# First key loads and packs split over two DMA queues, and two changes to a planner's clock, in an attention and mixture-of-experts kernel

## The chip, the cores and the metric

One Trainium2 chip, one of its cores. The metric is device time in microseconds (us) of one execution, as the median of several runs. Before the change it is 415.95 us, the median of 3 runs from 412.87 to 416.46.

## What is computed

There are 8 batches of 8 heads, 576 tokens and a head size of 64, all in float32. Per batch, 32 pack vectors `p` attend over keys `k` and values `v`, and then the queries `q` attend over the 32 packed results. The output of that, 576 x 512, goes through a mixture of 8 experts: one expert per token, two layers (512 to 1024 with a ReLU, 1024 to 512), scaled by the gate's probability.

```python
p_packed = softmax(scale * p @ k.T) @ v            # per batch and head, 32 x 64
x = softmax(scale * q @ p_packed.T) @ p_packed      # 576 x 64 per head, 576 x 512 per batch
logits = x @ w_gate; local = sigmoid(x @ w_local)
for s in range(576):                                # per batch
    fresh = argmax(logits[s])
    e = fresh if s == 0 or local[s] < 0.5 else e    # expert of this token
    out[s] = softmax(logits[s])[e] * (relu(x[s] @ w1[e]) @ w2[e])
```

The inputs are random, with `q`, `k` and `p` of spread 0.8 and small gate weights.

## The kernel before

**Work.** The kernel takes the expert of a batch's first token for the whole batch, counts tokens that would have another one, and has a branch behind the main program for those. Per batch, tokens are turned so that the head dimension lies on partitions; the scores of packs against keys are made (line 504), softened on VectorE and ScalarE (512 to 533), turned (542, 547), multiplied with the values (568) and turned again into `ppT` (589). Then come the scores of queries against `ppT` (619) and their softmax (654 to 686), which leaves the weights of the 32 packs for each token as a rounded part `a2h` and a rest `a2l`. The first layer's weights `w1` of the chosen expert are multiplied with `ppT` (941 for batch 0, in quarters; 970 for the others, in two halves of 512 columns), so that the first layer works on `a2h` and `a2l` directly (1012). Its result goes through ReLU into `h` (1023, 1027) and the second layer (1045, 1050, 1054), in 2 x 8 chunks a batch. Stores are at 1094.

**The order of the work.** It is written out when the program is built. Each piece is a generator that yields `need(...)`: the tiles it waits for, banks of PSUM and conditions. A planner, `weave`, keeps a clock of its own (`Clock`), whose `note` gives every emitted instruction a start and an end on its engine; a piece is taken when the clock says that what it needs is there, and the chunks (`main`) come when nothing of the attention pieces is due. As long as `warm_ps` is held, which is until batch 0's third chunk, a stretch in which the clock finds nothing ready is filled with multiplications of constants, `keep_warm` (line 228, tile `heat`), one for each 230 ns. Every engine runs its instructions in the order in which they were emitted; what they truly wait for are semaphores, which the clock does not decide.

**What the clock believes.** A DMA ends after its bytes over a rate, plus 2000 or 2500 ns (line 165). SP's and ScalarE's transfers are two lines that do not slow each other. A tile has one time of writing, or two where `halves` lists it; an instruction that writes a tile starts after the last write of it, by whatever engine, and after the last use.

**Around the change.** `loads` for batch 0 issues the packs (line 373: the same rows twice, to the left and the right half of `p_in`, one from SP and one from ScalarE), then the small inputs (299, 300, 302: two batches' first queries, `w_local`, `w_gate`, all from ScalarE), and then on SP the keys of Q 0 (347, in two pieces of two heads, and 349, the tail of 64 tokens, tile `qt`), the keys of Q 1, the values (330, 332) and the queries. Q numbers the two groups of four heads. `turn_tokens` turns keys: two groups of four transposes (449), copied to the tile `xT` (named `qn`) by ScalarE and by VectorE (451), one transpose of the tail (457) and its copy by ScalarE (459). The three copies write different columns. `turn_small` (309, 311) turns the small inputs and is taken once Q 0's keys are turned. `weights` loads `w1` (904 for batch 0, 920 for the others, two transfers of 1 MB each) and `w2` (891), once the expert is in a register. `pack_weights` (970) needs both halves of `w1`.

Of the kernel before, what the change touches and what calls it, by code (L numbers as in the profile page):

```python
# [19 lines left out]
B, H, S, D = 8, 8, 576, 64  # L20
# [5 lines left out]
NJ = 4  # L26
# [30 lines left out]
PICK = 2  # L57
# [3 lines left out]
class Clock:  # L61
# [3 lines left out]
    def __init__(self):  # L65
        self.until, self.written, self.used, self.before = {}, {}, {}, {}
        self.slots, self.done, self.group, self.tiled, self.products = {}, set(), (None, set()), False, 0.0

        self.halves = {}

        self.rate = 300.0

        self.port = {"DVE": [], "Pool": []}

# [58 lines left out]
    def note(self, inst):  # L133
        outs = [x.bass_ap for x in inst.outs if hasattr(x, "bass_ap")]
        ins = [x.bass_ap for x in inst.ins if hasattr(x, "bass_ap")]
        if inst.opcode == "TensorLoad":

            if "SP" in str(inst.engine):
                self.until["SP"] = self.ready([x for x in ins]) + 1000.0
        if not outs:  # L140
            return
        dma = inst.opcode == "DMACopy"
        if dma:
            aside = "Activation" in str(inst.engine)
            kind, took = "DMA2" if aside else "DMA", min(x.free_size() * x.partition_size() for x in outs + ins if x.space != DRAM) * 4 / self.rate
        else:
            kind, took = self.price(inst, outs, ins)
        start = max(self.engine(kind), self.engine("Activation" if aside else "SP") if dma else 0.0)
        for x in ins + ([] if dma else outs):
            at, by = self.written.get(self.key(x), (0.0, kind))  # L150
            start = max(start, at + (LAT if by != kind else 0.0 if kind == "PE" else SAME))
        for x in outs:
            t = x.tensor.name
            start = max(start, 0.0 if dma else self.used.get(self.key(x), 0.0))
            if t in self.before:
                start = max(start, self.used.get(self.before.pop(t), 0.0) + LAT)
        if kind == "Pool" or kind == "DVE" and inst.opcode in ("TensorTensor", "TensorScalar", "TensorScalarPtr") and not any(x.space == PSUM for x in ins + outs):
            for a, z in self.port["DVE" if kind == "Pool" else "Pool"][-8:]:
                if a <= start < z:
                    start = z  # L160
            self.port[kind].append((start, start + took))
        end = start + took
        self.until[kind] = end
        if dma:
            end += 2000.0 if start < 25000.0 else 2500.0
        for x in outs:
            self.written[self.key(x)] = (end, kind)
        for x in ins + outs:
            for t in {x.tensor.name, self.key(x)}:
                self.used[t] = max(end, self.used.get(t, 0.0))  # L170
# [3 lines left out]
def packed_attn_moe_kernel(  # L174
# [12 lines left out]
    nc = tc.nc  # L187
# [4 lines left out]
    clock = Clock()  # L192
    at_batch = [-1]

    def tile_(shape, dtype, name, tag=None):
        bufs = BUFS.get(tag or name, 2)
        x = sb.tile(shape, dtype, name=name, tag=tag or name, bufs=bufs)
        clock.follow(x.tensor.name, tag or name, bufs)
        return x
# [42 lines left out]
    small = const.tile([(PICK + 1) * H, D], F32, name="small")  # L242
# [53 lines left out]
    def load_small():  # L296

        clock.rate = 100.0
        nc.scalar.dma_start(out=small[0:PICK * H], in_=q[0:PICK, :, 0, :].rearrange("b h d -> (b h) d"))
        nc.scalar.dma_start(out=small[PICK * H:(PICK + 1) * H], in_=w_local.rearrange("(h d) e -> h (d e)", d=D))  # L300
        sts[0]["rows"] = tile_([128, DM], F32, "gate_rows", "w2raw")
        nc.scalar.dma_start(out=sts[0]["rows"][0:H], in_=w_gate.rearrange("(h d) e -> h (d e)", d=D))

    def turn_small():

# [29 lines left out]
    def load_pairs(st, name, Q):  # L335

        src, b, tag = (k if name == "k" else q), st["b"], "kv" if name == "q" and st["second"] else "w2s"
        x = tile_([128, HQ, NJ * D], F32, "kv" if tag == "kv" else "kw", tag)
        clock.halves[x.tensor.name] = HQ * NJ * D
        if Q == 0:  # L340
            st[name, "rest"] = tile_([128, NQ, 2 * D], F32, "qt", "o")
            clock.halves[st[name, "rest"].tensor.name] = NQ * 2 * D
        rest = st[name, "rest"][:, Q]
        rows = at(src, b).rearrange("(h q) s d -> q h s d", q=NQ)[Q]
        clock.rate = 300.0
        for hs in (slice(0, 2), slice(2, 4)) if st["early"] and (name, Q) == ("k", 0) else (slice(0, 4),):
            nc.sync.dma_start(out=x[:, hs], in_=rows[hs, 0:512].rearrange("h (p c) d -> p h (c d)", c=NJ))
        clock.rate = 200.0
        nc.sync.dma_start(out=rest, in_=rows[:, 512:S].rearrange("h (p r) d -> h p (r d)", r=2))
        return x, rest  # L350
# [17 lines left out]
    def load_packs(b, queues):  # L368

        x = tile_([128, 2, 2 * D], F32, "p_in")  # L370
        clock.rate = 400.0
        for z, queue in enumerate(queues):
            queue.dma_start(out=x[:, :, D * z:D * z + D], in_=at(p, b).rearrange("(g h) n d -> (h n) g d", g=2))
        return x
# [23 lines left out]
    def loads(st):  # L398

        b = st["b"]  # L400
        if st["early"]:
            st["px"] = load_packs(b, (nc.sync, nc.scalar))
            load_small()

            order = (("k", 0), ("k", 1), ("v", 0), ("v", 1), ("q", 0), ("q", 1))
        else:
            if isinstance(b, int):
                yield need(when=lambda: "loaded" in sts[b - 1] and (b < 2 or "ereg" in sts[b - 2]))
            order = (("k", 0), ("k", 1), ("p", 1)) if st["second"] else \
                (("v", 0), ("v", 1), ("p", 1), ("k", 1), ("q", 1))  # L410
        for name, Q in order:
            blocks = name in "kq" and not st["pairs"]
            if isinstance(b, int) and b > 1:
                yield need(when=lambda: all(len(sts[x].get(y, ())) == n for x, y, n in ((b - 2, "w2", NC), (b - 1, "w1", 2)) if "ereg" in sts[x]))
# [21 lines left out]
    def turn_tokens(st, name):  # L436
# [2 lines left out]
        yield need(slot="qn", when=lambda: (name, 0) in st and (early or ("a2t" in st if st["early"] else sts[0]["asked"] >= NQ)))  # L439
        xT = st[name] = tile_([128, NQ, HQ, HALF], F32, "qn")  # L440
        clock.halves[xT.tensor.name] = H * HALF
        for Q in range(NQ):
            yield need(when=lambda: (name, Q) in st and (early and (Q == 0 or st["scored"] > 0) or st["second"] or st["valued"] == NQ and (Q == 0 or st["ppT"][Q] is not None)))
            x, rest = st[name, Q]
# [436 lines left out]
    def weights(st):  # L881
# [34 lines left out]
        for fh in range(2):  # L916
            yield need(slot="w1t")
            clock.rate = 330.0
            w1t = tile_([128, HQ, 512], F32, "w1t")
            nc.sync.dma_start(out=w1t, in_=src[:, :, 512 * fh:512 * fh + 512])  # L920
            st["w1"].append(w1t)
        for c in range(NC):
            yield from second(c)
# [436 lines left out]
```

## Time and profile before

| what | value |
|---|---|
| median of 3 runs | 415.95 us (412.87 to 416.46) |
| time of the profiled execution | 415.69 us |
| its span in the trace | 413.9 us |
| TensorE (PE) busy | 405.7 us, 98% |
| VectorE (DVE) busy | 301.9 us, 73% |
| ScalarE (ACT) busy | 180.1 us, 44% |
| moved by DMA | 73.08 MB, mean 177 GB/s |
| mean granted TensorE clock | 0.998 of full speed |

Times in the trace count from the start of the span. PE are TensorE's multiplications, PEld its weight loads, which lie beside them; SPq and ACTq are the sequencers of SyncE and ScalarE, which issue DMAs. A line such as L970 is one of the kernel before. "Idle before" is the time that an engine stood still before an instruction, with what ended it. The chain of waits is the work that ended last, followed back step by step.

### The profile page before, as it was taken

What the parts mean: (1) busy time and instruction counts of PE and PEld (TensorE: products, weight loads), DVE (VectorE), ACT (ScalarE), POOL (GpSimd) and SP (SyncE); (2) the same over time, 40 slices, a digit from 0 to 9 for tenths busy, and PEclk for the clock granted to TensorE, in tenths of its full rate; (3) what the DMA queues carried; (4) which work ended last, traced back from release to release, by engine and by line L of the source; (5) the groups of instructions that cost most, each with busy time, mean ns of one, the idle gap of its engine ahead of it and who ended that gap; (6) DMA issues with size and microseconds to landing.
All of it is one profiled execution on the core that took longest, in us unless ns stands there. A gap on an engine that the chain in (4) does not pass through costs nothing.

```text
span 413.9 us, 10072 instructions
## 1 busy us (share of the span) xinstructions
PE 405.7 (98%) x3820; PEld 319.8 (77%) x3821; DVE 301.9 (73%) x905; ACT 180.1 (44%) x440; POOL 47.7 (12%) x67
## 2 busy tenths in 40 slices
PE   7999999999999999999999999999999999999995
PEld 4657787678868778788787788877787788878895
DVE  2498779895868949697588968878597976867231
ACT  2556543653436424446245443355244453454221
POOL 2003500641030000300002000300003000110000
PEclk9999999999999999999999999999999999999999
DMA  7869998999994997849994799938998400733021
GB/s 219 254 230 319 121 187 246 210 255 169 137 329 138 229 143 124 306 132 209 127 234 181 236 155 141 319 111 226 126 146 303 153 2 2 272 122 129 0 66 55
DMA packets 169325, 73.08 MB, mean 177 GB/s; under 512 B 135088, under 2 KB 149424, under 8 KB 169272
## 3 DMA queue, kind: packets, MB, share of 16 engines
q1 hardware_dynamic: 168792, 72.17, 79.9%
q8 instruction: 31, 0.51, 0.6%
q10 hardware_dynamic: 480, 0.22, 0.2%
q14 instruction: 22, 0.18, 0.2%
HBM read 62.94 MB, written 9.44 MB: 175 GB/s over the span
## 4 chain that ended last, share of the span: by engine, by line
PE 91%; DMA 5%; ACT 1%; SPq 1%; DVE 0%; issue 0%; DVEq 0%; ACTq 0%
PE bank L1045 41%; PE bank L1012 24%; DMA w1t<-in_moe_w_dram 4%; PE bank L1050 4%; PE bank L1054 4%; PE bank L970 3%; PE bank L568 2%; PE bank L504 2%; PE bank L619 2%; PE bank L542 2%; PE bank L228 2%; DMA qt<-in_k_dram 1%; PE bank L797 1%; PE bank L449 1%; PE bank L941 1%; PE bank L739 1%
## 5 line engine op out<-in xcount | busy, mean ns | idle before, releaser
L1045 PE MATMUL bank<-w2s,h 128*128 128x512 f32 (+1 forms) x792 | 204.6, 392 | 0.0
L1045 PEld LDWEIGHTS bank<-w2s,h 128*128 128x128 f32 x792 | 137.2, 188 | 25.8 <-issue 3.1
L1023 ACT ACTIVATE h<-bank 128x256 fp32r<-128x256 f32 (+1 forms) x128 | 52.7, 412 | 111.5 <-PE bank L1012 110.7
L1027 DVE SCALAR_TENSOR_TENSOR h<-bank,h 128x256 fp32r<-128x256 f32 x192 | 61.7, 349 | 52.7 <-ACT h L1023 51.1
L1012 PEld LDWEIGHTS bank<-a2h,wph 128*128 128x128 f32 x256 | 46.1, 188 | 19.7 <-issue 5.6
L686 POOL TENSOR_TENSOR a2l<-a2t,a2h 128x576 fp32r<-128x576 f32 (+2 forms) x17 | 24.1, 1419 | 300.6 <-ACT a2h L683 300.6
L1012 PE MATMUL bank<-a2h,wph 128*128 128x320 f32 (+1 forms) x256 | 56.5, 302 | 0.1
L1012 PE MATMUL bank<-a2h,wpl 128*128 128x320 f32 (+1 forms) x256 | 54.6, 294 | 0.0
L1012 PE MATMUL bank<-a2l,wph 128*128 128x320 f32 (+1 forms) x256 | 54.3, 293 | 0.0
L1012 PEld LDWEIGHTS bank<-a2h,wpl 128*128 128x128 f32 x256 | 40.8, 188 | 0.3
L1012 PEld LDWEIGHTS bank<-a2l,wph 128*128 128x128 f32 x256 | 40.8, 188 | 0.0
L998 ACT CAST w2s<-w2raw 128x512 fp32r<-128x512 f32 x64 | 38.5, 621 | 3.8 <-DMA w2raw<-in_moe_w_dram 3.8
L1000 DVE TENSOR_TENSOR w2s<-w2raw,w2s 128x512 fp32r<-128x512 f32 x50 | 33.3, 679 | 0.0
L1050 PE MATMUL bank<-w2s,h 128*128 128x512 f32 x64 | 26.9, 420 | 0.0
L1054 PE MATMUL bank<-w2s,h 128*64 128x512 f32 x64 | 25.2, 394 | 0.0
L985 DVE TENSOR_TENSOR wpl<-bank,wph 128x512 fp32r<-128x512 f32 x28 | 18.2, 682 | 7.8 <-ACT wph L982 7.8
L982 ACT CAST wph<-bank 128x512 fp32r<-128x512 f32 x28 | 15.1, 593 | 18.1 <-PE bank L970 18.1
L639 DVE STREAM_TRANSPOSE sT<-bank 128x288 f32<-128x288 f32 (+2 forms) x36 | 13.0, 418 | 9.7 <-ACT gate L637 9.0
L1000 POOL TENSOR_TENSOR w2s<-w2raw,w2s 128x512 fp32r<-128x512 f32 x14 | 18.1, 1309 | 14.1 <-ACT w2s L998 5.8
L603 DVE STREAM_TRANSPOSE qn<-qn 128x1152 f32<-128x1152 f32 x14 | 19.2, 1368 | 0.0
L471 DVE STREAM_TRANSPOSE qn<-qn 128x1152 f32<-128x1152 f32 x12 | 16.3, 1362 | 0.0
L512 DVE TENSOR_SCALAR_CACHE_REDUCE a<-bank 128x288 f32<-128x288 f32 x32 | 13.3, 453 | 3.0 <-PE bank L504 3.0
(158 smaller groups left out, 457.3 us busy)
## 6 DMA issues: line engine op xcount, KB each, us to landing
w2raw<-in_moe_w_dram SPq DMA_DIRECT2D x64, 256.0 KB, 5.7
w1t<-in_moe_w_dram SPq DMA_DIRECT2D x14, 1024.0 KB, 7.2
kv<-in_v_dram SPq DMA_DIRECT2D x16, 512.0 KB, 5.8
qn<-in_q_dram SPq DMA_DIRECT2D x28, 288.0 KB, 6.7
out_dram<-o SPq DMA_DIRECT2D x28, 256.0 KB, 3.5
qn<-in_k_dram SPq DMA_DIRECT2D x24, 288.0 KB, 7.4
w1t<-in_moe_w_dram SPq DMA_DIRECT2D x4, 512.0 KB, 4.7
out_dram<-o SPq DMA_DIRECT2D x14, 128.0 KB, 2.4
```

The lines of the kernel that those rows point to most:

```text
L471: nc.vector.transpose(out=kT, in_=kT)
L603: nc.vector.transpose(out=qT, in_=qT)
L686: eng.tensor_tensor(out=a2l, in0=a2t, in1=a2h.bitcast(F32), op=ALU.subtract)
L985: nc.vector.tensor_tensor(out=lo[fh][:, Q], in0=ts[fh, Q], in1=hi[fh][:, Q].bitcast(F32), op=ALU.subtract)
L998: nc.scalar.copy(out=w[:, 0], in_=raw)
L1000: (nc.gpsimd if st["pick"] and not st["early"] or st["early"] and c > 1 else nc.vector).tensor_tensor(out=w[:, 1], in0=raw, in1=w[:, 0].bi ...
L1012: nc.tensor.matmul(out=t[:, :GROUP * (m1 - m0)], lhsT=st["wp"][c // 4][wi][:, Q, fs], rhs=a2[ai][Q][:, GROUP * m0:GROUP * m1], start=(n == ...
L1023: nc.scalar.activation(out=h[:, :w], in_=t[:, :w], func=AF.Relu)
L1027: nc.vector.scalar_tensor_tensor(out=h[:, dst:dst + z - a], in0=t[:, a:z], scalar=0.0, in1=h[:, a:z].bitcast(F32), op0=ALU.max, op1=ALU.su ...
L1045: nc.tensor.matmul(out=acc[:, cols], lhsT=hs[hi], rhs=w[:, wi, cols], start=(c == 0 and n == 0), stop=(c == NC - 1 and n == 2),)
L1050: nc.tensor.matmul(out=acc, lhsT=h[:, 256:WIDE + TAIL], rhs=w[:, 0], start=(c == 0), stop=False, skip_group_check=True,)
L1054: nc.tensor.matmul(out=acc[0:TAIL], lhsT=h[:, 256:WIDE], rhs=w[:, 1], start=False, stop=(c == NC - 1), skip_group_check=True,)
```

## The change

The packs of batch 0 are both issued by ScalarE; of the first keys, SP issues the first two heads and ScalarE the other two. The small inputs move from ScalarE to SP, and from behind the packs to behind the keys of both groups, ahead of the values. In the planner's clock, tiles of turned tokens (`apart`) are no longer held back by the last write or use of the tile, and keep the latest of their writers' ends; and the two `w1` transfers of batches 1 and 2 are counted as landing 1500 ns later (`late`). No instruction of the arithmetic is added or removed.

```diff
-        self.halves = {}
-        self.rate = 300.0
+        self.halves, self.apart = {}, set()
+        self.rate, self.late = 300.0, 0.0
...
-        for x in ins + ([] if dma else outs):
+        for x in ins + ([] if dma else [y for y in outs if y.tensor.name not in self.apart]):
             at, by = self.written.get(self.key(x), (0.0, kind))
             start = max(start, at + (LAT if by != kind else 0.0 if kind == "PE" else SAME))
         for x in outs:
             t = x.tensor.name
-            start = max(start, 0.0 if dma else self.used.get(self.key(x), 0.0))
+            start = max(start, 0.0 if dma or t in self.apart else self.used.get(self.key(x), 0.0))
...
-            end += 2000.0 if start < 25000.0 else 2500.0
+            end += (2000.0 if start < 25000.0 else 2500.0) + self.late
+        for x in outs:
+            if x.tensor.name in self.apart:
+                end = max(end, self.written.get(self.key(x), (0.0, kind))[0])
...
     def load_small():
-        nc.scalar.dma_start(out=small[0:PICK * H], ...)            # and two more, 300 and 302
+        nc.sync.dma_start(out=small[0:PICK * H], ...)
...
-        for hs in (slice(0, 2), slice(2, 4)) if st["early"] and (name, Q) == ("k", 0) else (slice(0, 4),):
-            nc.sync.dma_start(out=x[:, hs], ...)
+        for queue, hs in ((nc.sync, slice(0, 2)), (nc.scalar, slice(2, 4))) if st["early"] and (name, Q) == ("k", 0) else ((nc.sync, slice(0, 4)),):
+            queue.dma_start(out=x[:, hs], ...)
...
         if st["early"]:
-            st["px"] = load_packs(b, (nc.sync, nc.scalar))
-            load_small()
+            st["px"] = load_packs(b, (nc.scalar, nc.scalar))
...
         for name, Q in order:
+            if st["early"] and (name, Q) == ("v", 0):
+                load_small()
...
         clock.halves[xT.tensor.name] = H * HALF
+        clock.apart.add(xT.tensor.name)
...
+            clock.late = 1500.0 if st["at"] in (1, 2) else 0.0
             nc.sync.dma_start(out=w1t, in_=src[:, :, 512 * fh:512 * fh + 512])
+            clock.late = 0.0
```

## Rows read from the trace of the kernel before

**Rows 1.** The page's first part: busy time, share of the span, instructions.

```profile
PE 405.7 (98%) x3820; PEld 319.8 (77%) x3821; DVE 301.9 (73%) x905; ACT 180.1 (44%) x440; POOL 47.7 (12%) x67
```

**Rows 2.** TensorE's waits over the span: total us, times, longest us.

```profile
PE bank L457 <- DMA qt<-in_k_dram: 0.9, 1, 0.9
PE bank L970 <- DMA w1t<-in_moe_w_dram: 0.9, 2, 0.6
```

**Rows 3.** Chain of waits, first 10 us: start us, length us, what.

```profile
0.88 0.46 SPq L373
...
1.90 0.47 SPq L347
2.41 4.98 DMA qt<-in_k_dram
```

**Rows 4.** Timeline, 4 to 12 us: start us, length us, engine, line, what.

```profile
4.67 1.82 PE L449 MATMUL bank<-ident,kw 128*128 128x128 f32 x8
...
6.54 0.69 DVE L451 COPY qn<-bank 128x512 f32<-128x512 f32 x1 [4.16 <-PE bank L449]
...
7.70 0.21 PE L309 MATMUL bank<-ident,small 24*64 24x24 f32 x1
...
7.80 0.27 ACT L459 COPY qn<-bank 128x128 f32<-128x128 f32 x1 [1.42 <-PE bank L457]
...
8.28 0.82 PE L228 MATMUL bank<-heat 128*128 128x512 bf16 x3
...
9.03 0.72 PE L504 MATMUL bank<-qn,pT 64*32 64x288 f32 x16
...
10.81 0.69 DVE L451 COPY qn<-bank 128x512 f32<-128x512 f32 x1
10.92 0.27 ACT L459 COPY qn<-bank 128x128 f32<-128x128 f32 x1
```

**Rows 5.** Timeline of SP's queue, around the first keys.

```profile
2.41 0.75 SPq L349 DMA_DIRECT2D qt<-in_k_dram  x1
...
3.26 0.38 SPq L347 DMA_DIRECT2D kw<-in_k_dram  x1
```

**Rows 6.** DMA issues of the first 8 us: KB each, median us to landing.

```profile
kv<-in_v_dram SPq DMA_DIRECT2D x2, 512.0 KB, 7.5
...
small<-in_q_dram ACTq DMA_DIRECT2D x1, 4.0 KB, 3.1
```

**Rows 7.** Busy time by stretch; the last two columns are DMA share, GB/s.

```profile
5.00:6.00 1.00, 1.00 (x7) 1.00 (x6) 0.00 (x0) 0.52 (x2) 0.00 (x0) 1.00 0.71 156
...
22.00:24.00 2.00, 2.00 (x25) 0.82 (x10) 1.67 (x6) 0.00 (x0) 0.00 (x0) 1.00 0.08 20
```

**Rows 8.** Timeline: the first layer's start, batch 0.

```profile
29.84 0.56 PE L1012 MATMUL bank<-a2h,wph 128*128 128x320 f32 x2
```

**Rows 9.** Timeline: line 970 of batch 1 and of batch 2, first halves.

```profile
72.68 1.09 PE L970 MATMUL bank<-w1t,ppT 64*32 64x512 f32 x16
...
121.74 1.09 PE L970 MATMUL bank<-w1t,ppT 64*32 64x512 f32 x16
```

**Rows 10.** Chain of waits: second halves of line 970, two chunks, a batch without wait.

```profile
74.11 1.09 PE bank L970 x16
75.20 0.90 PE bank L1012 x6
...
79.09 1.39 PE bank L1045 x6
...
81.17 1.39 PE bank L1045 x6
...
123.41 1.09 PE bank L970 x16
124.51 0.90 PE bank L1012 x6
...
173.06 1.88 PE bank L970 x32
```

More of the change, by code (lines that the diff above doesn't have):

```diff
@@ L298, in load_small @@
         clock.rate = 100.0
-        nc.scalar.dma_start(out=small[0:PICK * H], in_=q[0:PICK, :, 0, :].rearrange("b h d -> (b h) d"))
-        nc.scalar.dma_start(out=small[PICK * H:(PICK + 1) * H], in_=w_local.rearrange("(h d) e -> h (d e)", d=D))
+        nc.sync.dma_start(out=small[0:PICK * H], in_=q[0:PICK, :, 0, :].rearrange("b h d -> (b h) d"))
+        nc.sync.dma_start(out=small[PICK * H:(PICK + 1) * H], in_=w_local.rearrange("(h d) e -> h (d e)", d=D))
         sts[0]["rows"] = tile_([128, DM], F32, "gate_rows", "w2raw")
-        nc.scalar.dma_start(out=sts[0]["rows"][0:H], in_=w_gate.rearrange("(h d) e -> h (d e)", d=D))
+        nc.sync.dma_start(out=sts[0]["rows"][0:H], in_=w_gate.rearrange("(h d) e -> h (d e)", d=D))
     def turn_small():
@@ L345, in load_pairs @@
         clock.rate = 300.0
-        for hs in (slice(0, 2), slice(2, 4)) if st["early"] and (name, Q) == ("k", 0) else (slice(0, 4),):
-            nc.sync.dma_start(out=x[:, hs], in_=rows[hs, 0:512].rearrange("h (p c) d -> p h (c d)", c=NJ))
+        for queue, hs in ((nc.sync, slice(0, 2)), (nc.scalar, slice(2, 4))) if st["early"] and (name, Q) == ("k", 0) else ((nc.sync, slice(0, 4)),):
+            queue.dma_start(out=x[:, hs], in_=rows[hs, 0:512].rearrange("h (p c) d -> p h (c d)", c=NJ))
         clock.rate = 200.0
```

## The prediction

> **What bounds it now.** The page's busy table comes first: TensorE works 405.7 us of a span of 413.9, 98%, and the next engine, VectorE, 301.9 [rows 1]. So only three things move the end: time in which PE stands still, fill work that PE does, and the order of its work. PE's waits come second. Two groups concern this change: 0.9 us before line 457, for the tail of the first keys, and 0.9 us in two pieces before line 970, for `w1` of batches 1 and 2 [rows 2]. In the chain of waits the start hangs on SP: it issues the packs at 0.88 (0.46 us), then two pieces of keys, the second at 1.90 (0.47 us), then at 2.41 the tail `qt`, which needs 4.98 us to land [rows 3]. The timeline shows what hangs on that: the first key transposes end at 4.67 + 1.82 = 6.49, PE waits for the tail, ScalarE's copy ends at 7.80 + 0.27 = 8.07, and the scores begin only at 9.03, behind `turn_small` (7.70) and three multiplications of constants (0.82 us) that the planner put there [rows 4]. Everything up to the first layer at 29.84 [rows 8] follows from that start, in the order of PE's queue.
>
> **Part 1, the tail of the first keys lands earlier: worth 0.8 us.** SP loses one issue of packs and one of keys ahead of `qt`: 0.46 + 0.47 us and the gaps between them, so that `qt` goes out at 0.88 + 0.46 + 0.06 = 1.40 in place of 2.41, 1.01 us sooner [rows 3]. With an unchanged 4.98 us it lands at 6.38, before the transposes ahead of it end at 6.49. Line 457 then starts behind them, 0.9 us earlier: the whole wait of [rows 2] goes. What is late next is VectorE's copy of heads 2 and 3, which ends at 6.54 + 0.69 = 7.23, in place of ScalarE's at 8.07 [rows 4]: 0.84 us, and I take 0.8. The second pack copy goes out behind the first on ScalarE, half a microsecond later than from SP, and the second key half at about the old time; both are costed at nothing, as the transposes before the wait run from 4.67 without an idle gap. The transfers that the two issues are moved past gain too: SP's keys of Q 1, at 3.26 now, come a microsecond sooner [rows 5].
>
> **Part 2, the clock allows two writers: worth 0.4 us.** The clock had lined up the three copies of the keys. The trace shows that they need not: for Q 1 VectorE copies from 10.81 and ScalarE from 10.92, side by side [rows 4]. By its own rules the clock now has the first keys 0.3 us earlier, about one multiplication of constants at 230 ns; of the 0.82 us before line 504 I expect one or two of three to go. Bounds: nothing (if `turn_small` ends later than the keys, the fill is not on the path) and the full 0.82 us. I take 0.4, half of it. Nothing else in the kernel needs this copy's order, so the edit itself costs nothing.
>
> **Part 3, the small inputs on SP: taken at no cost, the weakest step.** They now stand behind four key issues and ahead of the values. At 0.38 to 0.75 us an issue [rows 5] the last of the three goes out at about 4.4 us, an estimate. The first of them took 3.1 us from issue to landing on the empty queue [rows 6], which gives 7.5 for the last. `turn_small` follows line 457 by some 0.3 us (7.39 to 7.70), so it would start at 6.8, and stands ahead of the scores on PE: it waits 0.7 us. Its transposes took 8.28 - 7.70 = 0.58 us [rows 4] and would end at 8.1, where the scores could have begun soon after the copies at 7.23. That takes back some of parts 1 and 2 together: of 1.2 us I keep 0.8 to 1.2, and take 1.0. The values go out about a microsecond later than they would have, near their old time; the list of PE's waits, of which [rows 2] are two, has none for them.
>
> **Is that start carried to the end?** Between 22 and 24 us the DMA engines move 20 GB/s at a share of 0.08 [rows 7]: they wait for the expert, which PE's chain delivers. The heavy loads start from there, so they shift with it. Behind 29.84 PE is busy without a gap except in the rows named, and a shift of 1.0 us stays a shift.
>
> **Part 4, later `w1` in the clock: worth 1.5 us.** In batch 1 the first half of line 970 starts at 72.68, the second waits until 74.11 and the next work begins at 75.20: 2.52 us. In batch 2 it is 121.74 to 124.51, 2.77 us. In a batch whose weights are there the same 32 multiplications take 1.88 us [rows 9, 10]. So the wait costs 0.64 + 0.89 = 1.53 us. Counted 1500 ns later, the piece comes one chunk later; a chunk takes 81.17 - 79.09 = 2.08 us [rows 10]. The start at 72.68 becomes 74.76, behind the end of the wait at 74.11, and 121.74 becomes 123.82, behind 123.41. Work to fill the gap is there: chunks of the older batch follow line 970 up to and past 81.17 [rows 10]. What is late next is the split of the packed weights, on ScalarE and VectorE: its second part starts 74.76 - 74.11 = 0.65 us later, and the chunks that follow line 970, over 6 us of PE's work up to 81.17, cover that. Bounds: two runs of 16 take 2 x 1.09 = 2.18 us against 1.88 in one, so that one more or one fewer change between kinds of work on PE is 0.3 us; the part lies between 0.3 us lost, where the waits stay and a change is added, and 1.5 + 0.3 gained. I take 1.5.
>
> **Sum.** 1.0 + 1.5 = 2.5 us off the profiled execution's 415.69, so 413.2 us. The median of the three runs is 415.95, 0.26 above it; 413.4 us is what I forecast for the median.
>
> **Rivals.**
>
> *The two queues share what moves data (10%).* If the first transfers are bound by data, the tail lands at 7.39 as before and only parts 2 and 4 pay: 415.95 - 1.5 - 0.4 = 414.1 us. Against it: from 5 to 6 us, with the tail still on its way, the engines move 156 GB/s at a share of 0.71 [rows 7], less than they can; the tail is late because it was issued late. The Trainium skill, "DMA: Bandwidth & Descriptors", section "Issuing engines are not separate DMA queues", says that DMAs of any issuing engine run on the same 16 DMA engines and interleave, and that issuing on several saves only the sequencers' time. Where the engines are full that leaves this rival's 414.1; the sum's 413.4 rests on the issue time alone, which the rule grants, and the 156 GB/s say that the engines were not full.
>
> *The planner's order comes out as before at line 970, or the weights land later still (13%).* SP's issue of batch 1's `w1` may shift less than PE. Then only the start pays: 415.95 - 1.0 = 414.9 us.
>
> *The start's gain is lost at `turn_small` (17%).* If the last small transfer lands at about 8.4, the scores begin at 9.0 as now, and only line 970 pays: 414.4 us.
>
> *A new and longer wait at `turn_small`, slower (12%).* The small inputs stand in SP's queue behind 576 KB of keys of Q 1 (four heads of 576 tokens), and PE runs in order: everything waits at line 309. Transfers of SP that wait behind others took 7.5 us to land [rows 6]: 4.4 + 7.5 = 11.9, and the scores, 1.33 us behind line 309 as now (9.03 - 7.70), begin at 13.2 instead of 9.03, 4.2 us late. Less 1.5 for line 970 that is 415.95 + 2.7 = 418.7 us. It decides from the point where the small inputs land later than 7.70 + 1.5 = 9.2. Against it: they are 22 KB, and the queue ahead of them is emptied sooner than before.
>
> *A better order (13%).* With fewer constants in several places up to 29.84 the start could gain 2.5 us, and with the 1.8 of part 4: 415.95 - 4.3, about 411.6 us. For it speaks that the chain there crosses fill work again and again; against it, that ScalarE's and VectorE's chains set most of those steps.
>
> The forecast itself has 35%, with its own range of 412.4 to 414.4.
>
> **Range and chances.** From 411.2, a little beyond the better order, to 416.6, which takes in the milder half of the slow case (from no gain to 418.7 less 2); beyond lie its worse half and an order that comes out worse for reasons that I can't see, 1 to 2 in 10. A measurement of this kernel can tell about 1% from no change, 4.2 us: faster means below 411.8, slower above 420.1. Only the better order reaches the first, and a little over half of it; the spread of the runs (412.87 to 416.46) may carry the forecast there too: 0.10 in all. Slower by over 1% needs more than the slow rival's 418.7, such as a wait for the values behind the other one: 0.05. Within: 0.85.
>
> **What would show it.** Line 457 at 6.5 without a DMA wait, line 504 at about 8.0, line 1012 first at about 28.8; line 970 of batches 1 and 2 as one run of 32 in 1.88 us without a wait for `w1t`. A wait of PE for `small` or `gate_rows` at line 309 would show part 3 wrong; two runs of 16 at line 970 would show part 4 wrong; a first layer at 29.8 in spite of earlier scores would show that the start isn't carried.

## The result and the profile after

The changed kernel is slower: 419.44 us in the median of five runs (418.70 to 421.25) against 415.85 of five runs of the kernel before (412.87 to 416.46), a ratio of 1.0102 with a 95% interval of 1.0058 to 1.0147. The forecast was 413.4. The profiled execution took 418.71 us with a span of 416.9, against 415.69 and 413.9, so the trace shows 3.0 of the 3.6 us.

TensorE's waits in the kernel after (total us, times, longest) answer to [rows 2]. Line numbers have moved: 309, 449, 457, 504, 542, 970, 1012 and 1027 are now 312, 454, 462, 509, 547, 977, 1019 and 1034.

```profile
PE bank L312 <- DMA small<-in_moe_w_local_dram: 1.3, 1, 1.3
PE bank L547 <- ACT a L538: 1.0, 1, 1.0
PE bank L454 <- DMA kw<-in_k_dram: 0.8, 1, 0.8
```

Both groups of [rows 2] are gone, the tail's and the weights'. Three others stand in their place. The timeline of the start (start us, length us, engine, line) shows two of them, and answers to [rows 4, 8]:

```profile
4.81 1.06 PE L454 MATMUL bank<-ident,kw 128*128 128x128 f32 x4
...
6.68 1.11 PE L454 MATMUL bank<-ident,kw 128*128 128x128 f32 x4 [0.81 <-DMA kw<-in_k_dram]
...
9.28 0.24 PE L312 MATMUL bank<-ident,small 24*64 24x24 f32 x1 [1.27 <-DMA small<-in_moe_w_local_dram]
...
10.61 1.21 PE L509 MATMUL bank<-qn,pT 64*32 64x288 f32 x16
11.75 1.97 PE L454 MATMUL bank<-ident,kw 128*128 128x128 f32 x8
...
14.58 0.71 PE L509 MATMUL bank<-qn,pT 64*32 64x288 f32 x16
...
32.57 0.56 PE L1019 MATMUL bank<-a2h,wph 128*128 128x320 f32 x2
```

The first scores start at 10.61 in place of 9.03, and they and the second group of key transposes take 1.21 and 1.97 us, where the later scores take 0.71. In the kernel before, the second group took 1.09, at the same place in the order:

```profile
9.68 1.09 PE L449 MATMUL bank<-ident,kw 128*128 128x128 f32 x8
```

The first layer starts 2.73 us late. The chain of waits names the transfer on which the start now hangs, as [rows 3] named the tail:

```profile
3.81 5.43 DMA small<-in_moe_w_local_dram
```

Further on, the chain shows the weights' gain and what took its place, and answers to [rows 10]:

```profile
77.48 1.88 PE bank L977 x32
...
90.25 6.56 DMA w2raw<-in_moe_w_dram
...
96.89 0.62 ACT w2s L1005
97.51 0.78 ACT a L538 x2
...
130.76 1.88 PE bank L977 x32
```

Line 977 runs as one group of 32 in both batches. But the exponentials of line 538 stand on ScalarE behind a cast of second-layer weights that waits for a transfer, and TensorE waits 1.0 us for them. (This is among batch 1's chunks, where batch 2's attention is worked in; "batch 2" below means this stretch.)

**Where the 3.0 us lie.** Line 1050 (1057 after) runs 8 times a batch, so its starts mark the batches. Up to line 1012 the kernel after loses 2.73; from there to batch 0's last chunk it gains 0.09; to batch 1's first chunk, with line 970 of batch 1, it gains 0.67 (24.63 to 23.96); to batch 2's first chunk it loses 0.61 (48.27 to 48.88); up to batch 7's last chunk there is nothing (0.01), and the last stretch loses 0.4, which is about what it differs by between two traces of one kernel (21.2 and 20.8 us in the kernel before, here and in experiment 7). The sum is 2.73 - 0.09 - 0.67 + 0.61 + 0.01 + 0.4 = 3.0.

### The profile page after: what moved, and what is told of

It is laid out like the page before. It is cut to its first block, busy times and chain, and to the rows that moved or that the text cites. A ratio compares the mean times of both kernels' runs of the same rounds, so it can differ in the third digit from the quotient of the medians.

```text
span 416.9 us, 10060 instructions
## 1 busy us (share of the span) xinstructions
PE 407.2 (98%) x3816; PEld 320.7 (77%) x3817; DVE 297.6 (71%) x905; ACT 180.2 (43%) x440; POOL 47.9 (11%) x67
## 4 chain that ended last, share of the span: by engine, by line
PE 92%; DMA 3%; ACT 1%; SPq 1%; issue 0%; POOL 0%; DVE 0%; ACTq 0%; DVEq 0%
PE bank L1052 43%; PE bank L1019 24%; PE bank L1057 4%; PE bank L1061 3%; PE bank L977 3%; PE bank L573 2%; PE bank L509 2%; PE bank L547 2%; PE bank L624 2%; PE bank L231 2%; DMA w2raw<-in_moe_w_dram 2%; DMA small<-in_moe_w_local_dram 1%; PE bank L454 1%; PE bank L802 1%; PE bank L948 1%; PE bank L744 0%
```

## The experiments

Theory A: the start is lost by the order of issues in the two queues (late key half, late small inputs), and the planner's two edits are good or neutral. Rivals: the order of TensorE's work, the sheer number of bytes, the clock alone.

**1. The queues alone, and the planner's edits alone.** The first is the changed kernel without the two edits of the clock, the second the kernel before with only these.

```
e1:  -        clock.apart.add(xT.tensor.name)
     -            clock.late = 1500.0 if st["at"] in (1, 2) else 0.0
e2:  -  ((nc.sync, slice(0, 2)), (nc.scalar, slice(2, 4)))   +  ((nc.sync, ...), (nc.sync, ...))
     -  load_packs(b, (nc.scalar, nc.scalar))                +  load_packs(b, (nc.sync, nc.scalar)); load_small()
     load_small(): nc.sync back to nc.scalar
```

> Only the DMA part of the change; the planner's clock as before, so TensorE's order is that of the kernel before. Theory A (the queues cost): line 449's second group waits some 0.8 us for the second key half and line 309 some 1.3 us for the small inputs, the slow multiplications last until about 13 us, the first layer starts at 32.3 to 33, and the time is 418 to 419.5 us. Theory B (the clock's new order costs, by taking away fill work): the first layer starts at 30.5 or earlier and the time is 416.5 us or less.

> Only the two clock edits; all DMAs on the queues of before, TensorE's order is that of the changed kernel. Theory A: the first layer starts at 29.0 to 29.9, line 970 runs as 32 in 1.88 us in batches 1 and 2, a wait of about 1 us before line 542 in batch 2 stays, and the time is 414.5 to 416 us. Theory B: the first layer starts at 31 or later and the time is 417.5 us or more.

The queues alone took 419.49 us (ratio 1.0084, 1.0053 to 1.0116), the planner's edits alone 415.39 (1.0008, 0.9982 to 1.0034). The whole loss is in the queues. TensorE's order in the first is that of before, and yet line 1012 starts at 34.96, 2 us beyond what I expected: the waits for the key half and the small inputs are 1.2 and 2.4 us. With the planner's edits alone it starts at 28.78, 1.06 us early, and the span is only 0.5 shorter: the rest is given back in batch 2, at a place I had not named, a wait of 0.9 us before the first layer for VectorE's `h`, and in batch 3, where a wait for weights turns up that before doesn't have (0.33 us at 173.43).

**2. Filling the idle time.** The changed kernel, with multiplications of constants that the planner does not count: 2 ahead of the second group of the first key transposes and 5 ahead of line 312.

```
+    def fill(n): clock.mute = True; keep_warm(n); clock.mute = False
...
+        fill(5)          # ahead of the first transpose of turn_small
...
+                if early and Q == 0 and n == 1: fill(2)
```

> The changed kernel with 2 more multiplications of constants ahead of the second group of key transposes and 5 ahead of the small inputs' transposes, which its clock doesn't count, so that all else keeps its order. They lie in TensorE's waits. Theory A (idle TensorE early on is why it ran at half speed until about 14 us): the scores' 16 multiplications take 0.65 us in place of 1.14 and the next 8 transposes 1.0 in place of 1.90, the first layer starts 1.0 to 1.5 us sooner, at 31.1 to 31.6, and the time is about 417.8 us. Rival C (the slow stretch comes from something else, such as data arriving): the same durations as in the changed kernel, the first layer at 32.6 or later.

```profile
11.39 0.72 PE L519 MATMUL bank<-qn,pT 64*32 64x288 f32 x16
12.04 1.09 PE L464 MATMUL bank<-ident,kw 128*128 128x128 f32 x8
...
31.88 0.56 PE L1029 MATMUL bank<-a2h,wph 128*128 128x320 f32 x2
```

The first scores (line 519 here) and the second key group (464) take 0.72 and 1.09 us again, full speed, and the first layer (1029) starts at 31.88, 0.69 earlier than in the kernel after although the scores start 0.78 later (11.39), and 0.3 later than I expected at the latest: 1.47 us of the loss between the two lines was TensorE's speed. The median of four runs is 418.01, its ratio of 1.0101 with an interval of 1.0018 to 1.0183 too wide to show a gain.

**3. The small inputs back on ScalarE's queue**, behind the key half.

```
load_small(): nc.sync back to nc.scalar; called right behind load_packs
```

> The changed kernel with the three small inputs back on ScalarE's queue, behind the packs and the second key half; orders of TensorE, VectorE and GpSimd unchanged. Theory A with the small inputs as the larger cost: the wait of 1.3 us before them goes, the scores begin at 8.8 to 9.4, the first layer at 30 to 31, the time is 416 to 417.3 us. Rival D (the second key half on ScalarE's queue is the larger cost): the scores begin at 10 or later and the time stays above 418 us.

416.84 us (1.0051, 1.0013 to 1.0089): about half of the loss is gone, though the interval overlaps that of the kernel after. The wait for the small inputs falls to 0.4, that for the key half grows to 1.5. TensorE still falls to the lower clock. Its timeline and, by stretch, its busy time (columns as in [rows 7]: TensorE's busy time is second, the granted clock third from the end):

```profile
9.35 1.21 PE L509 MATMUL bank<-qn,pT 64*32 64x288 f32 x16
10.49 1.97 PE L454 MATMUL bank<-ident,kw 128*128 128x128 f32 x8
```

```profile
6.00:9.00 3.00, 1.65 (x15) 1.26 (x15) 0.78 (x3) 0.41 (x2) 0.00 (x0) 0.86 0.97 288
9.00:12.00 3.00, 3.00 (x24) 1.74 (x24) 1.35 (x9) 0.36 (x1) 0.00 (x0) 0.50 0.95 289
12.00:15.00 3.00, 3.00 (x23) 0.92 (x21) 0.69 (x1) 1.29 (x4) 0.00 (x0) 0.50 1.06 319
```

The scores start only 0.32 us later than before, and line 1019 2.48 later (32.32, where I expected 30 to 31): here nearly all of the start's loss is the stretch at 0.50.

**4. The second key half back on SyncE's queue**, the small inputs still behind the keys there.

```
-  ((nc.sync, slice(0, 2)), (nc.scalar, slice(2, 4)))   +  ((nc.sync, slice(0, 2)), (nc.sync, slice(2, 4)))
```

> The kernel after, with the second half of the first keys back on SyncE's queue (both packs stay on ScalarE's, the small inputs stay on SyncE's behind the first keys). Theory A (the half came late because it was queued on ScalarE behind the packs): no wait of TensorE at the second group of the first key transposes, which run as 8 in one; the wait for the small inputs at line 312 stays (their place in SyncE's queue is the same, with 256 KB more ahead of them: 1.3 to 2.5 us), so that line 509 starts at 9.5 to 10.5 and the time is 416.5 to 418.5 us. Rival B (it is the sum of the bytes in flight, whichever queue issues them): the wait at the second key group stays at 0.8 to 1.5 us and the time at 419. If the clock gate answers to TensorE's early idle time, matmuls at half rate appear for a stretch here too, as the wait of 1.3 us or more is still there.

417.69 us (1.0050, 1.0023 to 1.0078). Its trace is of an execution of 421.87, far above its median, so only the sequence is read: no wait at the key group, 1.7 us for the small inputs, and the granted clock at 0.50 from 12 to 14. The order changed with the edit, which I had not expected: the planner puts the first scores ahead of line 312 (7.59 against 10.03). As expected, the half was late by its queue; the small inputs are the larger part.

**5. Only the packs moved**, with both edits of the planner: what the prediction's part 1 wanted from SyncE's queue.

```
as in 4, and load_small() on nc.scalar
```

> The kernel after, with the second key half on SyncE's queue and the small inputs back on ScalarE's: of the change in queues only the packs on ScalarE are left, with both edits of the planner's clock. Theory A (of the queue edits the key half and the small inputs cost the time, and the packs alone bring the tail forward, as the prediction had it): line 462 starts at about 6.9 without a DMA wait, line 509 at 7.5 to 8.0, line 1019 at 28.0 to 28.6, no stretch at the half clock; time 414.6 to 415.2 us, up to 0.8 below the kernel with the clock edits alone. Rival B (the packs' 256-byte packets on ScalarE's queue delay the small inputs behind them): wait of 0.5 us or more at line 312, no gain over the clock edits alone, 415.4 or more.

416.11 us (1.0024, 0.9996 to 1.0053): no gain over the planner's edits alone (415.39), so rival B's time, but not its mechanism: line 312 has no wait. The tail is no longer waited for (line 462 at 6.86), line 509 starts at 7.96, but line 1019 at 29.08. And batch 2 has the longest wait of its kind:

```profile
PE bank L1019 <- DVE h L1034: 2.3, 1, 2.3
...
PE bank L490 <- DMA p_in<-in_p_dram: 0.5, 1, 0.5
```

**6. Each edit of the planner by itself**, on the kernel before.

```
e7:  +  clock.late = 1500.0 if st["at"] in (1, 2) else 0.0     (no apart)
e8:  +  clock.apart.add(xT.tensor.name)                        (no late)
```

> The kernel before, with only the later landing of the first-layer weights of batches 1 and 2 in the planner's clock. Theory A (the mechanism at line 970 is right, and its gain is given back in batch 2 by changes of order): start as before (line 509 at 9.0, line 1019 at 29.8), the weight waits at line 977 gone, about 1.4 us ahead of before at the 8th chunk of the second layer, and at the 24th chunk only 0 to 0.6 us ahead, with a new wait of 0.5 to 1.1 us in batch 2; time 415.2 to 416.0 us. Rival B (the give-back in the kernel after came from its late start): the 1.4 us are kept to the end, 414.4 us.

> The kernel before, with only the two writers allowed in the planner's clock. Theory A (the start gains what it gained with both clock edits, and the weight waits at line 970 stay): line 504 at 8.2, line 1012 at 28.8, about 1.0 us ahead; the waits for the first-layer weights stay at 0.9 us or grow by as much as SyncE's loads do not follow; end 0.5 to 1.0 us ahead: 414.4 to 415.2 us. Rival B (weights land at a fixed time, so the lead is lost at line 970): the waits grow to 1.5 to 2.0 us and the end is as before, 415.4.

The later weights alone: 415.76 (1.0011, 0.9983 to 1.0040). No wait in batch 2 came here, so that theory A's sign of it failed; but the lead at batch 1's first chunk is 0.39 on the first trace of before and not 1.4 (1.31 on its second, below), and the time shows none. The two writers alone: 414.39 (0.9988, 0.9960 to 1.0016), line 1012 at 29.14, 0.70 early, and no wait for weights either, although nothing was done for them.

**7. The kernel before once more.**

> The kernel before, unchanged, profiled once more beside the others: what does its trace repeat? Theory A (the order sets the times from line 542 on, and an earlier tail of the first keys is lost by then, as the kernel with the late weights alone suggests): line 504 anywhere from 8.2 to 9.1 us, but line 542 at 12.3 to 12.6 and line 1012 at 29.7 to 29.9. Rival B (the start's time is carried): line 1012 moves with line 504. For line 970: if the wait for the first-layer weights is a matter of order it shows again at 0.6 to 1.0 us; if it is one execution's landing, it is 0 to 0.5.

415.45 us, span 413.6. The tail lands earlier than in the first trace, line 504 starts at 8.41 instead of 9.03, and line 542 still at 12.69, line 1012 at 29.98: what the first scores gain is not carried. What is late next are the keys of Q 1; the weights' wait is 0.5. Its waits:

```profile
PE bank L449 <- DMA kw<-in_k_dram: 0.5, 1, 0.5
...
PE bank L970 <- DMA w1t<-in_moe_w_dram: 0.5, 1, 0.5
PE bank L457 <- DMA qt<-in_k_dram: 0.3, 1, 0.3
```

**8. The kernel before without its opening multiplications of constants.**

```
-WARM, FILL = 6, 230.0
+WARM, FILL = 0, 230.0
```

> The kernel before without the six opening multiplications of constants, all else in the same order: TensorE stands idle until the packs land, and no transfer is changed. Theory A (early idle time of TensorE alone brings the half clock and costs what the kernel after lost beside its waits): the granted clock rises later than the 6.3 us of before, the first key transposes take 1.9 us or more, the first scores 1.2 us in place of 0.72, and line 1012 starts 0.8 to 2.0 us later than 29.84; time 416 to 417.5 us. Rival B (the clock's price is hidden behind the waits for data): line 1012 at 29.8 to 30.1 and 415.2 us.

Undecided. In the trace the key transposes take 1.97 and the scores 1.11, as at the lower clock, and line 1012 starts at 29.84 all the same, rival B: the next work waits for the keys of Q 1 anyway (0.7 us). But the median is 417.23 (1.0049, 1.0018 to 1.0080), as theory A had it. The traced execution, 415.24, is one of its two shortest, and cannot show where the others lose 2 us. That stays open.

**9. The key half ahead of the packs in ScalarE's queue**; these two lines are the only ones that move, on any engine.

```
-            st["px"] = load_packs(b, (nc.scalar, nc.scalar))
 ...
                 st[name, Q] = load_values(b, Q) if name == "v" else load_pairs(st, name, Q)
+                if st["early"] and (name, Q) == ("k", 0):
+                    st["px"] = load_packs(b, (nc.scalar, nc.scalar))
```

> The kernel after, with the second key half issued on ScalarE's queue ahead of the two pack copies instead of behind them; nothing else moves on any engine. Theory A (the half was late because it stood behind the packs in that queue): it lands by about 5.3 us, the wait at the second key group (0.8 to 1.5 us) is 0 to 0.2; the packs come up to 0.9 us later and line 490 waits for them; the small inputs land as before at about 9.2, so that their wait at line 312 grows by what the other wait loses, to 1.8 to 2.6 us, line 509 starts at about 10.6 again and the time is 418.5 to 419.5 us. Rival B (the two queues share what moves data, and the order within ScalarE's queue doesn't matter): the half lands at 6.2 us or later and the wait at the second group stays at 0.5 us or more.

```profile
PE bank L490 <- DMA p_in<-in_p_dram: 1.9, 1, 1.9
...
PE bank L312 <- DMA small<-in_moe_w_local_dram: 0.4, 1, 0.4
```

The wait for the half is gone, that for the packs is 1.9 us, and line 509 starts at 10.62, within 0.01 of the kernel after; 418.57 us (1.0109, 1.0063 to 1.0154). The queue's order decides which of them is late, and the small inputs, unmoved, set line 312 at 9.33 in either case. I had expected their wait to grow; the packs took the time before it.

**10. The small inputs ahead of the keys of Q 1 in SyncE's queue.** On SyncE three issues and two change places, and no instruction of another engine moves.

```
-            if st["early"] and (name, Q) == ("v", 0):
+            if st["early"] and (name, Q) == ("k", 1):
                 load_small()
```

> The kernel after, with the three small inputs ahead of the keys of Q 1 on SyncE's queue instead of behind them; only the order of SyncE's issues changes. Theory A (they were late because 576 KB of keys stood ahead of them in the queue): they are issued from 2.2 us on, land by 7.5, the wait at line 312 is 0 to 0.3 us, line 509 starts at 9.0 to 9.4; the keys of Q 1 come about 1.4 us later, near where before had them, and cost nothing; the wait at the second key group stays (0.8 to 1.5 us), line 1019 starts at 30.0 to 31.3 and the time is 416.0 to 417.3 us. Rival B (the DMA engines are full, and what lands late is a matter of bytes): the wait at line 312 stays at 1 us or more, and the time at 418 or more.

414.88 us (0.9987, 0.9957 to 1.0016): the loss is gone. The timeline:

```profile
5.05 1.69 PE L454 MATMUL bank<-ident,kw 128*128 128x128 f32 x8
...
6.78 0.21 PE L312 MATMUL bank<-ident,small 24*64 24x24 f32 x1
...
7.68 0.71 PE L509 MATMUL bank<-qn,pT 64*32 64x288 f32 x16
8.55 1.06 PE L454 MATMUL bank<-ident,kw 128*128 128x128 f32 x8 [0.16 <-PE bank L509]
...
28.61 0.56 PE L1019 MATMUL bank<-a2h,wph 128*128 128x320 f32 x2
```

Line 1019 starts 3.96 us earlier than in the kernel after: 2.50 up to line 312 (9.28 to 6.78), of which the two waits are 2.08 (0.81 and 1.27), and 1.46 from there to line 1019 (23.29 to 21.83), which I put down to the clock: the scores and the second key group alone take 0.71 and 1.06 here and 1.21 and 1.97 there, 1.41 us. The key half's wait, which I expected to stay, is gone too: with the keys of Q 1 issued at 3.66 and not at 2.21 the half lands 4.2 us after its issue and not 4.8. DMA issues of the first microseconds, first the kernel after, then this one (KB, us to landing):

```profile
kw<-in_k_dram ACTq DMA_DIRECT2D x1, 256.0 KB, 4.8
```

```profile
kw<-in_k_dram ACTq DMA_DIRECT2D x1, 256.0 KB, 4.2
```

**11. The same without the later weights.**

```
experiment 10, and  -            clock.late = 1500.0 if st["at"] in (1, 2) else 0.0
```

> The kernel after with the three small inputs ahead of the keys of Q 1 on SyncE's queue, and without the later landing of the first-layer weights in the planner's clock; TensorE's order is then that of the kernel with the two writers alone. Theory A (the later landing buys the weight waits and gives them back as waits on VectorE's h or ScalarE's a in batch 2): no such wait here, line 1019's first start near 28.6 as with the late weights, waits for the first-layer weights of 0 to 0.9 us, and the end 0.3 to 1.0 us below the kernel with the late weights: 413.8 to 414.6 us. Rival B (the late weights pay what the prediction said): the weight waits of 0.9 us or more return and the time is 415.4 to 416.4 us.

414.07 us (0.9971, 0.9943 to 0.9999): the only version whose interval lies below the kernel before, by 0.3%, and only just; of thirteen intervals here one may do that by chance, so a gain isn't shown. Line 1018 (1012 before) starts at 28.93, no wait for weights, none in batch 2, span 411.4 against 413.2 with the edit.

**12. The changed kernel once more.**

> The kernel after, unchanged, profiled once more: what does its trace repeat? Theory A (its loss sits in the start, in SyncE's queue and TensorE's clock): the wait for the small inputs at line 312 at 1.0 to 1.7 us, line 454's second group and line 509 at the half clock, line 1019 at 32.2 to 32.9 us; the wait before line 547 in batch 2 either repeats or turns up at line 1019, as the landing of single transfers falls. Rival B (that trace was an odd one): line 1019 below 31.5 us.

418.83 us, span 417.0; waits of 2.2 for the small inputs and 0.6 for the key half, the first layer at 33.96, 1.1 beyond what was expected, no wait before line 547. One line behind the first wait, its stretches, and under them those of experiment 10:

```profile
6.84 0.66 PE L454 MATMUL bank<-ident,kw 128*128 128x128 f32 x4 [0.58 <-DMA kw<-in_k_dram]
```

```profile
6.00:9.00 3.00, 1.03 (x7) 0.53 (x5) 0.69 (x1) 0.88 (x2) 0.00 (x0) 1.00 0.99 286
9.00:12.00 3.00, 2.22 (x26) 0.98 (x26) 0.43 (x4) 0.00 (x0) 0.00 (x0) 0.61 1.07 282
12.00:15.00 3.00, 2.78 (x18) 2.22 (x12) 1.69 (x6) 1.16 (x3) 0.00 (x0) 0.50 1.05 300
15.00:18.00 3.00, 3.00 (x26) 1.21 (x25) 1.18 (x6) 0.94 (x5) 0.00 (x0) 0.75 0.96 260
```

```profile
6.00:9.00 3.00, 2.79 (x36) 1.84 (x36) 1.69 (x8) 0.90 (x2) 0.00 (x0) 1.00 1.01 289
9.00:12.00 3.00, 2.95 (x32) 1.85 (x32) 1.97 (x8) 1.65 (x5) 0.00 (x0) 1.00 1.08 295
12.00:15.00 3.00, 2.94 (x52) 1.74 (x51) 1.71 (x8) 1.92 (x7) 0.00 (x0) 1.00 1.11 308
```

Here four transposes take 0.66 at 6.84, full speed, where the first trace of the kernel after has 1.11 at 6.68. TensorE works 1.03 of the 3 us from 6 to 9, and after that it is granted 0.61 and 0.50 of its 2.4 GHz, the lower level of 1.2 GHz; in experiment 10 it works 2.79 and keeps 1.00. The DMA engines move 286 and 289 GB/s in the same 3 us: not the amount but the order differs.

**13. The queues alone, with the small inputs ahead**: TensorE's order of before.

```
experiment 11, and  -        clock.apart.add(xT.tensor.name)
```

> The kernel before with the change of the queues alone, but the small inputs ahead of the keys of Q 1: TensorE's and VectorE's order are those of before, so it prices the tail's earlier landing by itself. Theory A (the tail comes about 1 us earlier and what is late next are the keys of Q 1, which landed at 8.8 to 9.5 us in the traces with the old queues and 8.4 us with this one): line 504 at 7.9 to 8.5, no wait for the small inputs, line 1012 at 29.1 to 29.5 us, time 414.7 to 415.3 us. Rival B (the fixed order of constants and copies behind the first scores eats the gain): line 542 at 12.4 or later, line 1012 at 29.7 to 30.0, 415.4 us. Rival C (the prediction's part 1, carried whole): line 1012 at 28.8 to 29.0.

```profile
PE bank L453 <- DMA kw<-in_k_dram: 1.5, 2, 0.8
```

```profile
12.79 0.75 PE L546 MATMUL bank<-ident,a 128*128 128x128 f32 x4
...
30.08 0.56 PE L1017 MATMUL bank<-a2h,wph 128*128 128x320 f32 x2
```

415.20 us (1.0009, 0.9978 to 1.0039), rival B's numbers by theory A's mechanism: line 508 at 8.49, line 546 at 12.79, the first layer at 30.08. The keys of Q 1 landed at 9.75 here and not at 8.4, and TensorE waited 0.7 for them and 0.8 for the key half: what the tail gains is lost to these two.

**The later weights over all traces.** Two stretches, by the starts of line 1050: a, from batch 0's last chunk to batch 1's first; b, from batch 1's first to batch 2's first.

| Traces | a, us | b, us |
|---|---|---|
| without the edit: before, experiments 7, 8, 13, 1 (queues), 6 (two writers), 11 | 24.63, 24.76, 24.08, 24.09, 24.92, 24.38, 24.07 | 48.27, 47.45, 47.45, 47.44, 47.44, 47.45, 47.44 |
| with it: after, experiments 12, 1 (planner), 5, 6 (weights), 10, 9, 2, 3, 4 | 23.96 in all ten | 48.88, 48.02, 48.81, 50.20, 47.65, 49.30, 48.27, 47.65, 47.64, 51.55 |

The edit takes 0.1 to 1.0 us from a, and adds 0.2 to 2.8 to b (4.1 in the disturbed trace of experiment 4), where six of the seven traces without it agree within 0.01 (the seventh, the first trace of before, has the longer wait of [rows 2], 0.58 us). The sum of both isn't lowered: it runs from 71.51 to 72.90 without the edit and, experiment 4 aside, from 71.60 to 74.16 with it.

## Why the prediction was wrong

**Part 3 failed, the step that I called the weakest.** It took the small inputs at no cost, with a wait of 0.7 us from an issue at 4.4 and 3.1 us to landing, the price of a transfer on an empty queue. The issues came when estimated (the second at 3.81, the last at 4.25), but the second needed 5.43 us and not 3.1: ahead of it in the queue stood the 576 KB that only my slow rival counted. So line 312 started at 9.28, not at 7.5. Moving the three issues ahead of these two brings 2.50 us up to line 312 (experiment 10), the key half's wait included. The Trainium skill, "DMA: Bandwidth & Descriptors", section "Two DMAs through the same engine are not ordered", says that within one queue of a DMA engine descriptors start in order; the runs agree, since the same bytes in another order bring the first layer 3.96 us sooner.

**Part 1 failed in "the second key half at about the old time", costed at nothing.** Issued at 1.86 in place of 1.90, it landed after 4.8 us, behind the packs in its queue and beside the keys of Q 1, and split the transposes: 0.81 us of waiting. In the other half of part 1 the mechanism was right (no wait for the tail is left), and its worth wrong: 0.8 forecast, nothing measured at the first layer with the old order (experiments 7 and 13: 29.98 and 30.08), 0.2 with the new (28.61 against 28.78; 28.93 against 29.14), about as much as two traces of before differ (29.84 and 29.98). I named VectorE's copy as late next; it was the keys of Q 1.

**What I did not see was the clock.** The kernel starts at the lower level, 1.2 GHz: before, the first eight transposes take 1.82 us [rows 4] and the next eight 1.09. TensorE stood idle in the new waits, and the lower level lasted longer or came back. In the first trace of the kernel after it never left before about 13.7 us: the transposes at 4.81 and 6.68 take 1.06 and 1.11 for four, and those at 11.75 still 1.97 for eight. In the second (experiment 12) it had left by about 7 and came back in the wait of 2.2 us. The work that bounds the start takes up to twice as long there. From line 312 to the first layer that cost 1.46 us by experiment 10; from the scores on it was 1.03 by the same experiment (21.96 to 20.93) and 1.47 by experiment 2. Not every wait does it: the 0.93 us ahead of line 457 before, and the 0.8 and 0.7 of experiment 13, were followed by work at full speed. My sum priced a wait at its length.

**Part 2 was right in kind, and larger**: 0.70 (experiment 6) to 1.06 us (experiment 1) for the 0.4 taken, on either side of its upper bound of 0.82; one constant instead of three ahead of the first scores, three instead of five ahead of the next.

**Part 4: the mechanism was right, its worth mis-sized.** Both groups of 32 run in 1.88 us. But 1.53 us was the price in one execution, with 0.9 us of waits [rows 2]: the second trace of before waits 0.5, two with its order not at all (experiments 8 and 13). And that "the chunks that follow line 970" cover the later split overlooked batch 2: there, by the chains of waits, work stands behind `w2raw` and an output's landing on ScalarE and VectorE, in a different place each time (line 547 or line 1019), and returns 0.2 us or more.

**Is the start carried?** From the first layer on, yes, and that made it dear: 2.73 us at the first layer, 3.0 at the end; by the second traces of both kernels (experiments 7 and 12) 3.98 and 3.4.

**The rivals.** The slow one had the right place, line 312, and the right transfer, and its point of decision was met: the wait ended at 9.28, against 9.2. It had the scores 4.2 us late; they came 1.58 late, and the clock and part 4's lost gain did the rest, so that its 418.7 stands near the measured 419.44 by two errors that cancel. I gave it 12%, because the small inputs are 22 KB, "and the queue ahead of them is emptied sooner than before", and the range ended at 416.6, short of its time. That was the error behind the number: what counted was what stood ahead in the queue; that the transfer was small didn't help it. The rival of two queues that share what moves data fell: line 462, which needs the tail, starts at 6.57 without a wait in experiment 10, against 7.43 and 6.82, behind waits, in the two traces of before.

## What to carry to other kernels

A move of a transfer to another queue is priced by what is then ahead of it, with the landing time of a transfer that stands behind as much, not of one on an empty queue; a small input that everything waits for goes ahead of bulk data that is used later. Near the start a wait of TensorE can cost more than its length, because the clock may rise later or fall behind it, so read the granted clock, and the durations, behind every new wait. And a wait of well under 1 us that hangs on one transfer should be seen in a second execution before a planner is tuned to it.

## What the runs showed of the hardware

- The clock column doesn't show every stretch at the lower level. In the first trace of the kernel after it shows 1.00 all through, while scores took 1.21 in place of 0.71; in the second, with the same durations, it shows 0.50. The first is a level that had not risen yet, and the column shows 1.00 for such a stretch in the kernel before too (the eight transposes in 1.82 us at 4.67); what it showed in the second is a fall. The durations tell it in both.
- A tiny instruction of VectorE can last as long as one of GpSimd's. In experiment 10 line 861, on 128 x 5 elements, took 1.29 us, during GpSimd's run of three from 86.65 on, and 0.17 at most its seven other times in that trace; line 858 just ahead of it took 1.23 against 0.20. In experiment 11 line 861 took 0.17 at a time when GpSimd stood idle. It lies on the way to the wait of 1.4 us in batch 2, and in experiment 5, with 1.28 us, on the way to that of 2.3. The rows, first of experiment 10, then of experiment 11:

```profile
86.65 3.77 POOL L1007 TENSOR_TENSOR w2s<-w2raw,w2s 128x512 fp32r<-128x512 f32 x3 [3.00 <-PE bank L1019]
86.77 1.23 DVE L858 TENSOR_TENSOR ex<-ex,sel 128x40 f32<-128x40 f32 x1
...
87.92 1.29 DVE L861 TENSOR_SCALAR gz<-gz 128x5 f32<-128x5 f32 x1
89.13 1.36 DVE L608 STREAM_TRANSPOSE qn<-qn 128x1152 f32<-128x1152 f32 x1
...
90.56 0.51 DVE L1034 SCALAR_TENSOR_TENSOR h<-bank,h 128x256 fp32r<-128x256 f32 x2
...
91.22 0.53 PE L1019 MATMUL bank<-a2h,wph 128*128 128x320 f32 x2 [1.42 <-DVE h L1034]
```

```profile
88.46 0.17 DVE L861 TENSOR_SCALAR gz<-gz 128x5 f32<-128x5 f32 x1
```

The Trainium skill, "SBUF — State Buffer", section "SBUF: two separate sides", says that VectorE, in its modes with two ports or with two inputs in SBUF, and GpSimd share a pair of ports, which whoever starts first holds for its whole instruction. The trace agrees as far as 1.29 us is about the length of one of the three GpSimd instructions (3.77 / 3 = 1.26) and the same line is short without one beside it; which mode line 861 ran in no trace shows.
